# Six weight tiles decoded by an integer addition, ScalarE passes bound to set places, and two foldings split by VectorE

## The chip, the cores and the metric

The kernel runs on one core of one Trainium2 chip. The metric is the device time of one execution in microseconds. Of before three executions were timed: 1432.74, 1432.77 and 1434.7 us, median 1432.77.

## The reference

Attention over eight batches and eight heads, with keys and values first condensed to 32 memory slots, and behind it two feed-forward layers:

```python
a = exp(phi - max(phi, axis=2)); a = a / (sum(a, axis=2) + 1e-9)
k_m = einsum('bhsm,bhsd->bhmd', a, k)
v_m = einsum('bhsm,bhsd->bhmd', a, v)
scores = (q @ k_m.T) / sqrt(64)
attn = softmax(scores)                      # over 32 slots
x = (attn @ v_m) as [4608, 512]
g = x @ w_gate;  x = (silu(g) * (x @ w_val)) @ w_out      # 512 -> 1536 -> 512
h = x @ w_in;    out = elu(h) @ w_out2                     # 512 -> 2048 -> 512
```

q, k, v are 8 x 8 x 576 x 64, phi is 8 x 8 x 576 x 32. The weights come to the chip as 64-bit floating-point words, seen as pairs of 32-bit words.

## The kernel before

The kernel is written in a tile framework: Python functions record instructions, and a scheduler sets the order in which they stand on each engine, by data dependences, by `tc.high_priority()`, and by `tc.issue_after(x)`, which keeps what is recorded in it behind instruction x. Once built, that order is fixed: each engine takes its own list row by row, and waits at a row until the rows of other engines that it needs have ended.

Every matrix product of the feed-forward layers is taken in two parts, an upper part rounded to a short format and the remainder, as three products (upper by upper, upper by lower, lower by upper). So a value that goes into them is split: ScalarE copies it rounded (hi), VectorE subtracts that from it (lo).

Stage 1, some 340 us, goes over the eight batches. Per batch there are front tasks (`phi`: maximum and exponentials of phi; `a_T`: transpositions of them on TensorE into `ps_aT`, copied by ScalarE to `a`, L348 and L342; `kv_mm` and `kv_T`: the condensed keys and values) and back tasks for each half of the batch's positions (`score`; `soft` and `norm`: a softmax on VectorE with its exponential L424 on ScalarE; `attn`: a transposition L451 and the split of the weights into `at`, hi L453 on ScalarE and lo L454 on VectorE). `vw` folds the values into the gate and value weights on TensorE (`pvw`, L237) and splits the result (`vw`, hi L242 on ScalarE, lo L243 on VectorE). `gate1` and `val1` then make the hidden units (`pg` and `pv`, L255 to L257; the gate's activation `s` L279 on ScalarE and L280 on VectorE; `h` L287, split into `hh` L266 and `hl` L268), and `down1` multiplies them with the output weights (`pd`, L260 to L262; copied out by ScalarE L542 and sent to memory, L543). The loop over batches records these products, and `tick()` puts tasks of the next batches, from the list `todo`, between them. Two foldings stand before the loop's own list: (0, 0) ahead of it, (0, 1) within its first products. Stages 2 and 3 are long runs of products from about 340 us on.

The weight tiles are decoded from 64-bit words (`words`): ScalarE takes the upper 32-bit word as a float and scales it (L126), which sets the exponent; VectorE shifts it by three (L127), puts the sign back (L128), makes the word's power of two (L130), scales the lower word by it (L131), and the sum is L144. The output-weight tiles are also split (L171 to L173). `later()` keeps the early decodes behind given instructions. Six tiles are decoded ahead of some 65 us: four gate tiles, two of them in halves, and two output-weight tiles.

The foldings (0, 0) and (0, 1) are split without VectorE, for `NEG` is 1: ScalarE copies one half rounded (L246), TensorE adds its product with the negated identity `minus` (L247), ScalarE copies the remainder (L248). Ahead of folding (0, 1) `spin` puts thirteen products that nobody reads (L300) on TensorE.

Of the kernel before, what the change touches and what calls it, by code (L numbers as in the profile page):

```python
# [8 lines left out]
F32 = mybir.dt.float32  # L9
F32R = mybir.dt.float32r  # L10
I32 = mybir.dt.int32
# [15 lines left out]
UA = 4  # L27
# [4 lines left out]
NSET = (NU1 - UA) // 2  # L32
NKV = 5
NQ = 3
NEG = 1


@with_exitstack
def attention_moe_moe(ctx: ExitStack, tc: tile.TileContext, qT, phiT, kv, kv4, w1g, w1o, w2, out):
# [81 lines left out]
    def words(v, r):  # L121
# [9 lines left out]
        stt(out=cf, in0=lo32.bitcast(U32), scalar=2.0 ** -52, in1=cf, op0=ALU.mult, op1=ALU.mult)  # L131
        return cf

    def later():
        st = ExitStack()
        for after in last.get("h"), first.get("ex"):
            if after:
                st.enter_context(tc.issue_after(after.ins))
        return st

    def load_w(v, r):
        with later():
            cf = words(v, r)
            last["sum"] = tt(out=v, in0=v, in1=cf, op=ALU.add)  # L144

# [3 lines left out]
    def load_wg(p, k2, pool, parts=1):  # L149
        t = pool.tile([128, 2, 512], F32, tag="w", name="wg")  # L150
        WG[p][2 * k2], WG[p][2 * k2 + 1] = t[:, 0], t[:, 1]
        r = raw.pop((p, k2), None)
        if r is None:
            r = fetch_w(w1g[p, k2])
        t = t.rearrange("p i c -> p (i c)")
        n = 1024 // parts
        for i in range(parts):
            cs = slice(n * i, n * i + n)
            load_w(t[:, cs], r[:, cs])
        ahead((p, k2))  # L160

    def load_wo(u2, pool):
        hi = pool.tile([128, 2, 512], F32R, tag="w", name="woh")
        lo = (bk_p if u2 else pool).tile([128, 2, 512], F32R, tag="w", name="wol")
        for i in range(2):
            WO[2 * u2 + i] = hi[:, i], lo[:, i]
        hi, lo = (x.rearrange("p i c -> p (i c)") for x in (hi, lo))
        v = work("wv")
        with later():
            cf = words(v, fetch_w(w1o[u2]))  # L170
            act(out=hi, in_=v, func=AF.Copy)  # L171
            tt(out=v, in0=v, in1=hi.bitcast(F32), op=ALU.subtract)
            tt(out=lo, in0=v, in1=cf, op=ALU.add)  # L173

    SET = {}
    stores = []
# [53 lines left out]
    def vw(b, p, pool=None, ps=None):  # L230
        t = VW[b, p] = vx_p.tile([128, 2, 2, 512], F32R, tag="vx", name="vw")
        both = ps or pool.tile([128, 2, 512], F32, tag="at", name="pvw")
        ps = [both[:, g] for g in range(2)]

        def head(j, g):
            r, c = slice(64 * g, 64 * g + 64), slice(32 * j, 32 * j + 32)
            return mm(ps[g][c], lhsT=Bs[b].vt[r, j, :], rhs=WG[p][j][r], start=True, stop=True)  # L237

        together([lambda j=j, g=g: head(j, g) for j in reversed(range(KD)) for g in (1, 0)])
        if b >= NEG or p >= UA // 2:  # L240
            with tc.high_priority() if pool is None else nullcontext():
                act(out=t[:, 0], in_=both, func=AF.Copy)  # L242
                tt(out=t[:, 1], in0=both, in1=t[:, 0].bitcast(F32), op=ALU.subtract)  # L243
            return
        for g in range(2):
            act(out=t[:, 0, g, :], in_=ps[g], func=AF.Copy)  # L246
            mm(ps[g], lhsT=minus, rhs=t[:, 0, g, :], start=False, stop=True, skip_group_check=True)  # L247
            act(out=t[:, 1, g, :], in_=ps[g], func=AF.Copy)  # L248

    def up1(ps, w, c0, at, s0):  # L250
        cs, ss = slice(c0, c0 + 128), slice(s0, s0 + HS)
# [19 lines left out]
    def gate1(b, u, at, s0, silu):  # L271
        pg = ps_gv.tile([128, HS], F32, tag="g", name="pg")
        up1(pg, VW[b, u // 2], 256 * (u % 2), at, s0)
        s = t_p.tile([128, HS], F32, tag="s", name="s")
        if silu:
            last["gate"] = act(out=s, in_=pg, func=AF.Silu)
        else:

            act(out=s, in_=pg, func=AF.Tanh, scale=0.5)  # L279
            stt(out=s, in0=s, scalar=1.0, in1=pg, op0=ALU.add, op1=ALU.mult)  # L280
        return s

# [19 lines left out]
    class Batch:  # L302
# [18 lines left out]
        def phi(self):  # L321
            ph = self.ph
            nmx = fr_p.tile([128, 2], F32, tag="nmx", name="nmx")
            nc.vector.tensor_reduce(out=nmx, in_=ph, op=ALU.max, axis=AX.X, negate=True)
            sm = fr_p.tile([128, 2], F32, tag="sm", name="sm")
            for g in range(2):
                act(out=ph[:, g, :], in_=ph[:, g, :], func=AF.Exp, bias=nmx[:, g:g + 1],
                    accum_out=sm[:, g:g + 1])
            self.rs = fr_p.tile([128, 2], F32, tag="rs", name="rs", bufs=2)
            nc.vector.tensor_scalar_add(out=self.rs, in0=sm, scalar1=1e-9)  # L330
            nc.vector.reciprocal(out=self.rs, in_=self.rs)
# [3 lines left out]
        def a_T(self, c0):  # L335
            if c0 == 0:
                self.a = fr_p.tile([128, 9, 128], F32, tag="a", name="a")
            ps = ps_fr.tile([128, 4, 128], F32, tag="at", name="ps_aT")
            ph = self.ph.rearrange("p g s -> p (g s)")
            if c0 == 4:  # L340
                nc.tensor.transpose(out=ps[:, 0], in_=ph[:, 512:640], identity=ident)
                act(out=self.a[:, 8], in_=ps[:, 0], func=AF.Copy)  # L342
                return
            for i in range(2):
                for g in range(2):
                    s0 = 128 * (c0 + i) + 640 * g
                    nc.tensor.transpose(out=ps[:, 2 * i + g], in_=ph[:, s0:s0 + 128], identity=ident)
            act(out=self.a[:, 2 * c0:2 * c0 + 4], in_=ps, func=AF.Copy)  # L348


        def kv_mm(self, cs, start, stop):
# [22 lines left out]
        def kv_T(self):  # L374
            ps = ps_fr.tile([128, 2, 4, M], F32, tag="at", name="ps_kvT")
            for i in range(2):
                nc.tensor.transpose(out=ps[:, i].rearrange("p j m -> p (j m)"),
                                    in_=self.kvm[:, i].rearrange("p g d -> p (g d)"), identity=ident)
            self.kT = bk_p.tile([128, 4, M], F32, tag="kT", name="kT", bufs=2)
            act(out=self.kT, in_=ps[:, 0], func=AF.Copy)  # L380
            if self.b == 0:
                self.kTd = bk_p.tile([128, 4, 2, M], F32, tag="kTd", name="kTd")
                nc.gpsimd.memset(self.kTd, 0.0)
                for g in range(2):
                    r = slice(64 * g, 64 * g + 64)
                    act(out=self.kTd[r, :, g], in_=ps[r, 0], func=AF.Copy)
            self.vt = vt_p.tile([128, 4, M], F32, tag="vt", name="vt")
            act(out=self.vt, in_=ps[:, 1], func=AF.Copy)

# [43 lines left out]
        def attn(self, hf):  # L435
            if hf == 0:
                self.at = av_p.tile([128, 2, 2, S], F32R, tag="at", name="at")
            if self.b == 0 and hf == 1:
                t = ps_at.tile([128, 2, T], F32, tag="at", name="ps_ex")
                sc = self.sc.rearrange("p g s -> p (g s)")  # L440
                for i in range(2):
                    for g in range(2):
                        c0 = 256 * i + 128 * g
                        nc.tensor.transpose(out=t[:, g, 128 * i:128 * i + 128], in_=sc[:, c0:c0 + 128], identity=ident)
                for g in range(2):
                    c0 = 512 + M * g
                    last["ex"] = nc.vector.transpose(out=t[:, g, 256:HS], in_=sc[:, c0:c0 + M])
                t = t[:, :, :HS]
            else:
                t = bk_p.tile([128, 2, HS], F32, tag="ex", name="ex")  # L450
                last["ex"] = nc.vector.transpose(out=t.rearrange("p g s -> p (g s)"), in_=self.sc.rearrange("p g s -> p (g s)"))  # L451
            hi, lo = (self.at[:, i, :, HS * hf:HS * hf + HS] for i in range(2))
            act(out=hi, in_=t, func=AF.Copy)  # L453
            tt(out=lo, in0=t, in1=hi.bitcast(F32), op=ALU.subtract)  # L454

        def store_at(self):
# [99 lines left out]
    for b in range(B):  # L556
# [1 line left out]
        bk = list(back_tasks(b + 1)) if b + 1 < B else []  # L558
        fr = list(front_tasks(b + 2)) if b + 2 < B else []
        if b == 0:  # L560
            wo = [lambda u=u: load_wo(u, wo_p) for u in range(UA // 2)]
            pair = last["sum"]

            def phi1():
                with tc.issue_after(pair.ins):
                    Bs[1].phi()
                load_q(Bs[1])

            f1 = [phi1] + list(front_tasks(1)) + [lambda: Bs[2].phi()]
            for i in range(max(len(wo), len(f1))):  # L570
                todo += wo[i:i + 1] + f1[i:i + 1]
        if 2 <= b <= 5:
            bk += [lambda: load_wg(2 + (b - 2) // 2, b % 2, wa_p)]
        if b == B - 2:
# [29 lines left out]
        for hf in range(2):  # L604
            for u in range(UA):
# [2 lines left out]
                hs[hf, u] = val1(b, u, Bs[b].at, HS * hf, s, silu)  # L608
                tick()
                if (b, hf, u) == (0, 0, 1):  # L610
                    with tc.issue_after(last["pe"].ins):
                        spin(ps_kv, "at", 13)
                    vw(0, 1, G2)
                if prev:
                    down1(*prev.pop(0))
# [495 lines left out]
```

## Time and profile before

| | |
|---|---|
| median of 3 executions | 1432.77 us |
| the profiled execution | 1434.9 us, its span 1433.1 us |
| TensorE (PE) busy | 1407.0 us, 98% |
| weight loads (PEld) | 1215.3 us |
| VectorE (DVE) busy | 1141.3 us, 80% |
| ScalarE (ACT) busy | 857.7 us, 60% |
| chain that ended last | PE 89%, DMA 5%, DVE 4% |

Busy time is the time in which an engine works at an instruction; the span goes from the first instruction to the last, and 1.8 us of the profiled execution lie around it. The chain that ended last is followed back from the last instruction, at each step to what released it. TensorE's records overlap: a product's record is longer than its distance from the next, which is seen from the starts.

### The profile page before, as it was taken

Reading aid. Unit: us, or ns where it says so; the run is one execution under the profiler, and the core shown is the slowest. Engines: PE = TensorE matmul, PEld = TensorE weight load, DVE = VectorE, ACT = ScalarE, POOL = GpSimd, SP = SyncE. Lnnn points to the kernel's source line nnn. Section 1 sums busy time; section 2 is a strip of 40 time slices with the busy share of each in tenths; the row PEclk is TensorE's granted clock in tenths of the full one; section 3 lists DMA queues with packets and bytes.
Section 4 is the critical chain, followed back from the end, with each engine's and each line's share of the span. In section 5 each row is a group of like instructions: output and inputs, shape, how many; then the busy total and the mean of one; then the engine's idle time right before and its main releaser. Section 6 shows DMA issues by size and latency. Waiting matters only on the chain.

```text
span 1433.1 us, 23220 instructions
## 1 busy us (share of the span) xinstructions
PE 1407.0 (98%) x9269; PEld 1215.3 (85%) x9269; DVE 1141.3 (80%) x1460; ACT 857.7 (60%) x1251; POOL 44.8 (3%) x73
## 2 busy tenths in 40 slices
PE   5999999999999999999999999999999999999998
PEld 4688889988999999999998888888888888888887
DVE  7998887778798886886978578894898488957884
ACT  4665545544466465465657388556866588549843
POOL 0000000000000000000000000000000000000000
PEclk7999999999999999999999999999999999999999
DMA  9887522663789988888889866766676667666653
GB/s 379 316 316 282 193 75 101 220 231 136 259 248 294 298 235 253 255 246 275 280 270 367 279 203 209 268 212 198 204 272 210 202 205 250 228 205 205 208 204 132
DMA packets 89484, 337.65 MB, mean 236 GB/s; under 512 B 9376, under 2 KB 23712, under 8 KB 70048
## 3 DMA queue, kind: packets, MB, share of 16 engines
q1 hardware_dynamic: 55312, 254.04, 51.4%
q10 hardware_dynamic: 26880, 51.39, 9.8%
q0 software_dynamic: 7184, 30.74, 8.9%
q8 instruction: 73, 1.20, 0.3%
q14 instruction: 35, 0.29, 0.1%
HBM read 251.13 MB, written 85.00 MB: 235 GB/s over the span
## 4 chain that ended last, share of the span: by engine, by line
PE 89%; DMA 5%; DVE 4%; issue 1%; ACT 1%; SPq 0%; ACTq 0%; DVEq 0%
PE pu L834 12%; PE pu L833 12%; PE pu L832 12%; PE pd L834 5%; PE pd L833 5%; PE pd L832 5%; PE acc L262 4%; PE acc L260 4%; PE acc L261 4%; PE pv L255 3%; PE pg L255 3%; PE pv L257 3%; PE pv L256 3%; PE pg L257 3%; PE pg L256 3%; DMA wr<-w1g 3%
## 5 line engine op out<-in xcount | busy, mean ns | idle before, releaser
L834 PE MATMUL pu<-xhi,w 128*128 128x512 f32 x672 | 261.5, 389 | 0.0
L833 PE MATMUL pu<-xlo,w 128*128 128x512 f32 x672 | 261.4, 389 | 0.0
L832 PE MATMUL pu<-xhi,w 128*128 128x512 f32 x672 | 261.4, 389 | 0.0
L861 ACT ACTIVATE xhi<-g 128x1024 fp32r<-128x1024 f32 x120 | 126.6, 1058 | 108.4 <-PE pu L834 65.9
L862 DVE TENSOR_TENSOR xlo<-g,xhi 128x1024 fp32r<-128x1024 f32 x120 | 145.2, 1222 | 42.2 <-ACT xhi L861 42.1
L833 PEld LDWEIGHTS pu<-xlo,w 128*128 128x128 f32 x672 | 126.1, 188 | 26.3
L832 PEld LDWEIGHTS pu<-xhi,w 128*128 128x128 f32 x672 | 126.1, 188 | 26.2
L834 PEld LDWEIGHTS pu<-xhi,w 128*128 128x128 f32 x672 | 126.1, 188 | 26.1
L261 PE MATMUL acc<-hh,ws 128*128 128x288 f32 x448 | 131.8, 296 | 0.0
L260 PE MATMUL acc<-hh,ws 128*128 128x288 f32 x448 | 131.5, 295 | 0.0
L262 PE MATMUL acc<-hl,ws 128*128 128x288 f32 x448 | 128.8, 297 | 0.0
L255 PE MATMUL pv<-at,vw 128*128 128x288 f32 x384 | 116.9, 304 | 3.0 <-DVE s L280 1.2
L255 PE MATMUL pg<-at,vw 128*128 128x288 f32 x384 | 116.5, 303 | 1.9 <-ACT at L453 0.7
L722 ACT ACTIVATE hh<-gh 128x576 fp32r<-128x576 f32 x112 | 76.1, 684 | 67.6 <-PE acc L261 50.3
L257 PE MATMUL pv<-at,vw 128*128 128x288 f32 x384 | 114.2, 297 | 0.0
L256 PE MATMUL pg<-at,vw 128*128 128x288 f32 x384 | 114.0, 297 | 0.2 <-DVE at L454 0.2
L256 PE MATMUL pv<-at,vw 128*128 128x288 f32 x384 | 114.1, 297 | 0.0
L257 PE MATMUL pg<-at,vw 128*128 128x288 f32 x384 | 113.8, 297 | 0.1
L832 PE MATMUL pd<-xhi,w 128*128 128x512 f32 x288 | 112.0, 389 | 0.0
L833 PE MATMUL pd<-xlo,w 128*128 128x512 f32 x288 | 112.0, 389 | 0.0
L834 PE MATMUL pd<-xhi,w 128*128 128x512 f32 x288 | 112.0, 389 | 0.0
L852 DVE SCALAR_TENSOR_TENSOR et<-et 128x1024 f32<-128x1024 f32 x72 | 87.9, 1221 | 28.8 <-ACT et L851 28.8
(154 smaller groups left out, 3240.4 us busy)
## 6 DMA issues: line engine op xcount, KB each, us to landing
w<-dnd SPq DMA_DIRECT2D x64, 1024.0 KB, 5.0
w<-upd SPq DMA_DIRECT2D x40, 1024.0 KB, 5.7
w<-upd SPq DMA_DIRECT2D x32, 768.0 KB, 4.7
ws<-d1d SPq DMA_DIRECT2D x42, 512.0 KB, 5.0
kvr<-kv SPq DMA_DIRECT2D x32, 512.0 KB, 8.2
wr<-w SPq DMA_DIRECT2D x16, 1024.0 KB, 6.3
upd<-uw ACTq DMA_DIRECT2D x32, 512.0 KB, 6.3
dnd<-uw ACTq DMA_DIRECT2D x32, 512.0 KB, 9.1
```

The lines of the kernel that those rows point to most:

```text
L255: mm(ps, lhsT=wh, rhs=ah, start=g == 0, stop=False)
L256: mm(ps, lhsT=wh, rhs=al, start=False, stop=False)
L257: last["pe"] = mm(ps, lhsT=wl, rhs=ah, start=False, stop=g == 1)
L260: mm(ps, lhsT=w[0][:, ms], rhs=hs[0], start=start, stop=False, skip_group_check=skip)
L261: mm(ps, lhsT=w[1][:, ms], rhs=hs[0], start=False, stop=False, skip_group_check=skip)
L262: mm(ps, lhsT=w[0][:, ms], rhs=hs[1], start=False, stop=stop, skip_group_check=skip)
L832: mm(ps, lhsT=w[0], rhs=x[0], start=start, stop=False, skip_group_check=skip)
L833: mm(ps, lhsT=w[0], rhs=x[1], start=False, stop=False, skip_group_check=skip)
L834: last["mm"] = mm(ps, lhsT=w[1], rhs=x[0], start=False, stop=stop, skip_group_check=skip)
L852: stt(out=a, in0=e, scalar=1.0, in1=a, op0=ALU.add, op1=ALU.mult)
L861: last["hi"] = act(out=hi, in_=x, func=AF.Copy)
L862: last["lo"] = tt(out=lo, in0=x, in1=hi.bitcast(F32), op=ALU.subtract)
```

## The change

`words_int` decodes the early tiles: ScalarE makes two passes, one over the upper words as before (L139 in the changed file) and one that turns the lower words into integers (L141); VectorE shifts the first (L142), adds the second as integers (L143) and puts the sign on by and/or (L144). An output-weight tile is then split by ScalarE (L189) and one VectorE row (L190). `BEHIND` binds the ScalarE passes to named instructions: behind an exponential, the `a` copy, `vt`, `at`. `NEG` is 0, so the first two foldings are split like all others (L259 on ScalarE, L260 on VectorE), and the split of every folding of stage 1 is recorded behind the last `ex`. `spin` is no longer called. In the first batch's `todo` the output weights are fetched apart from their decode.

```diff
-NEG = 1
+NEG = 0
...
+    def words_int(v, r, one, two):
+        lo32, hi32 = r[:, :, 0], r[:, :, 1]
+        vi = v.bitcast(I32)
+        n = work("wn").bitcast(I32)[:, :r.shape[1]]
+        with tc.issue_after(last[one].ins) if one else nullcontext():
+            act(out=v, in_=hi32.bitcast(F32), func=AF.Copy, scale=2.0 ** -112)
+        with tc.issue_after(last[two].ins) if two else nullcontext():
+            act(out=n, in_=lo32.bitcast(U32), func=AF.Copy, scale=2.0 ** -29)
+        nc.vector.tensor_scalar(out=vi, in0=vi, scalar1=3, scalar2=None, op0=ALU.logical_shift_left)
+        tt(out=vi, in0=vi, in1=n, op=ALU.add)
+        return stt(out=vi, in0=hi32, scalar=-2 ** 31, in1=vi, op0=ALU.bitwise_and, op1=ALU.bitwise_or)
...
+    BEHIND = {(0, 0): [(None, None), (None, "exp")], (0, 1): [(None, "a2"), (None, None)],
+              (1, 0): [("vt", "vt")], (1, 1): [("at", "at")]}
...
-            cf = words(v, fetch_w(w1o[u2]))
+            words_int(v, raw.pop(("wo", u2)), *[("exp", "s")[u2]] * 2)
             act(out=hi, in_=v, func=AF.Copy)
-            tt(out=v, in0=v, in1=hi.bitcast(F32), op=ALU.subtract)
-            tt(out=lo, in0=v, in1=cf, op=ALU.add)
+            tt(out=lo, in0=v, in1=hi.bitcast(F32), op=ALU.subtract)
...
-            with tc.high_priority() if pool is None else nullcontext():
-                act(out=t[:, 0], in_=both, func=AF.Copy)
+            with tc.high_priority() if pool is None else tc.issue_after(last["ex"].ins):
+                last["vw"] = act(out=t[:, 0], in_=both, func=AF.Copy)
                 tt(out=t[:, 1], in0=both, in1=t[:, 0].bitcast(F32), op=ALU.subtract)
...
-            wo = [lambda u=u: load_wo(u, wo_p) for u in range(UA // 2)]
+            wo = [lambda: (load_wo(0, wo_p), fetch_wo(1)), lambda: load_wo(1, wo_p)]
...
-            for i in range(max(len(wo), len(f1))):
-                todo += wo[i:i + 1] + f1[i:i + 1]
+            todo += [lambda: fetch_wo(0), f1[0], lambda: None, wo[0], f1[1], f1[2], wo[1]] + f1[3:]
...
                 if (b, hf, u) == (0, 0, 1):
-                    with tc.issue_after(last["pe"].ins):
-                        spin(ps_kv, "at", 13)
                     vw(0, 1, G2)
```

The order of the built programs, first on ScalarE in the first batch, from the gates' activations of the first half to the second `a` copy (`ph`: exponentials of phi for batch 1; `wv`, `wn`: decode passes of an output-weight tile; `wr`: its fetched words; `woh`: its upper part). Before:

```order
L266 ACTIVATE hh<-h 128x288
L327 ACTIVATE ph,sm<-ph,nmx 128x576 x2
L266 ACTIVATE hh<-h 128x288
L246 ACTIVATE vw<-pvw 128x512
L348 ACTIVATE a<-ps_aT 128x512
L248 ACTIVATE vw<-pvw 128x512
L246 ACTIVATE vw<-pvw 128x512
L453 ACTIVATE at<-ps_ex 128x2x288
L348 ACTIVATE a<-ps_aT 128x512
```

And now:

```order
L344 ACTIVATE ph,sm<-ph,nmx 128x576 x2
L139 ACTIVATE wv<-wr 128x1024
L141 ACTIVATE wn<-wr 128x1024
L283 ACTIVATE hh<-h 128x288
L259 ACTIVATE vw<-pvw 128x1024
L365 ACTIVATE a<-ps_aT 128x512
L470 ACTIVATE at<-ps_ex 128x2x288
L365 ACTIVATE a<-ps_aT 128x512
```

Two decode passes now stand between the exponentials and the folding's split; before, the tile's one pass stood ahead of the exponentials.

Second, ScalarE some 40 us later, within the first batch's down products, where batch 2's phi is transposed (`a`) and batch 1's second half goes through its softmax (`sc`, `at`; `p`: down products on their way out). Before:

```order
L348 ACTIVATE a<-ps_aT 128x512
L543 DMA p1d_124<-p_894 128x288
L424 ACTIVATE sc<-sc 128x576
L542 ACTIVATE p_957<-pd 128x288
L348 ACTIVATE a<-ps_aT 128x512
L543 DMA p1d_124<-p_957 128x288
L453 ACTIVATE at<-ex 128x2x288
L242 ACTIVATE vw<-pvw 128x1024
L266 ACTIVATE hh<-h 128x288
L279 ACTIVATE s<-pg 128x288
L342 ACTIVATE a<-ps_aT 128x128
```

And now:

```order
L365 ACTIVATE a<-ps_aT 128x512
L441 ACTIVATE sc<-sc 128x576
L559 ACTIVATE p_1007<-pd 128x288
L560 DMA p1d_124<-p_1007 128x288
L470 ACTIVATE at<-ex 128x2x288
L259 ACTIVATE vw<-pvw 128x1024
L365 ACTIVATE a<-ps_aT 128x512
L296 ACTIVATE s<-pg 128x288 x2
L359 ACTIVATE a<-ps_aT 128x128
```

The second `a` copy of four transpositions stood ahead of `at` and the split, and now stands behind both.

Third, TensorE at the same place, around the last transposition of batch 2's phi (`ps_aT<-ident,ph` of 128x128 alone). Before:

```order
L255 MATMUL pv<-at,vw 128x288
L256 MATMUL pv<-at,vw 128x288
L257 MATMUL pv<-at,vw 128x288
L341 MATMUL ps_aT<-ident,ph 128x128
L260 MATMUL pd<-hh,woh 128x288
L261 MATMUL pd<-hh,wol 128x288
```

And now:

```order
L274 MATMUL pv<-at,vw 128x288
L428 MATMUL ps_sc<-qr,kT 32x288 x8
L272 MATMUL pg<-at,vw 128x288
L273 MATMUL pg<-at,vw 128x288
L274 MATMUL pg<-at,vw 128x288
L272 MATMUL pg<-at,vw 128x288
L273 MATMUL pg<-at,vw 128x288
L274 MATMUL pg<-at,vw 128x288
L358 MATMUL ps_aT<-ident,ph 128x128
L272 MATMUL pv<-at,vw 128x288
```

The transposition that needs the second copy done followed the value products, with down products behind it; now a score and the gate products of one unit stand right ahead of it, and value products behind it.

## Rows read from the trace of the kernel before

**Rows 1.** Windows: from:to and its length, then busy time of each engine, clock, DMA.

```profile
60.00:100.00 40.00, 39.21 (x492) 30.24 (x492) 40.00 (x81) 24.54 (x56) 0.00 (x0) 0.98 0.93 346
100.00:200.00 100.00, 99.47 (x1113) 85.32 (x1113) 83.29 (x164) 54.48 (x128) 0.00 (x0) 1.00 0.58 206
400.00:1400.00 1000.00, 999.76 (x5588) 863.56 (x5588) 797.17 (x881) 638.05 (x815) 39.52 (x58) 1.00 0.74 243
```

**Rows 2.** Windows of 10 us, the same columns.

```profile
30.00:40.00 10.00, 8.80 (x34) 7.56 (x33) 10.00 (x14) 2.80 (x6) 0.00 (x0) 0.61 1.03 409
40.00:50.00 10.00, 8.37 (x127) 6.29 (x129) 9.58 (x19) 7.25 (x16) 0.00 (x0) 1.00 0.46 166
```

**Rows 3.** Source views of the decode lines: minimum, median and maximum in ns.

```profile
L126 ACT ACTIVATE wg<-wr x14: 658/1132/1161, 5.1 to 325.1; 128x1024 f32<-128x1024 f32 x10, 128x512 f32<-128x512 f32 x4
...
L127 DVE TENSOR_SCALAR wc<-wg x14: 419/686/694, 5.8 to 326.3; 128x1024 int32<-128x1024 int32 x10, 128x512 int32<-128x512 int32 x4
...
L144 DVE TENSOR_TENSOR wg<-wg,wc x14: 684/1219/1225, 9.6 to 331.3; 128x1024 f32<-128x1024 f32 x10, 128x512 f32<-128x512 f32 x4
```

**Rows 4.** Timeline of TensorE: start, duration, then the instruction.

```profile
36.37 3.80 PE L300 MATMUL spin<-minus 128*128 128x512 f32 x13
40.22 1.09 PE L237 MATMUL pvw<-wg,vt 64*32 64x512 f32 x16
...
43.68 0.29 PE L255 MATMUL pg<-at,vw 128*128 128x288 f32 x1
```

**Rows 5.** Timeline of VectorE and ScalarE around the second folding.

```profile
38.28 1.23 DVE L144 TENSOR_TENSOR wg<-wg,wc 128x1024 f32<-128x1024 f32 x1
...
45.80 0.75 DVE L454 TENSOR_TENSOR at<-ps_ex,at 128x576 fp32r<-128x576 f32 x1
...
42.72 0.58 ACT L246 ACTIVATE vw<-pvw 128x512 fp32r<-128x512 f32 x1
```

**Rows 6.** Timeline of TensorE: the groups of products later, by their starts.

```profile
74.48 0.72 PE L411 MATMUL ps_sc<-qr,kT 64*32 64x288 f32 x16
75.13 0.40 PE L260 MATMUL pd<-hh,woh 128*128 128x288 f32 x1
...
76.83 0.60 PE L347 MATMUL ps_aT<-ident,ph 128*128 128x128 f32 x4
77.36 1.09 PE L237 MATMUL pvw<-wg,vt 64*32 64x512 f32 x16
78.38 0.40 PE L255 MATMUL pg<-at,vw 128*128 128x288 f32 x1
...
80.06 0.28 PE L341 MATMUL ps_aT<-ident,ph 128*128 128x128 f32 x1
```

**Rows 7.** Timeline of ScalarE at the second excerpt's place.

```profile
77.19 0.69 ACT L424 ACTIVATE sc<-sc 128x576 f32<-128x576 f32 x1 [1.60 <-DVE sc L423]
...
78.07 0.59 ACT L348 ACTIVATE a<-ps_aT 128x512 f32<-128x512 f32 x1
...
78.91 0.69 ACT L453 ACTIVATE at<-ex 128x576 fp32r<-128x576 f32 x1 [0.25 <-DVE ex L451]
79.50 1.01 ACT L242 ACTIVATE vw<-pvw 128x1024 fp32r<-128x1024 f32 x1
```

**Rows 8.** Timeline of VectorE: rows of one softmax.

```profile
79.80 0.84 DVE L416 STREAM_TRANSPOSE sc<-ps_sc 128x288 f32<-128x288 f32 x2
...
82.40 0.74 DVE L422 TENSOR_REDUCE mx<-sc 128x18 f32<-128x576 f32 x1
83.06 0.26 DVE L431 RECIPROCAL smx<-smx 128x18 f32<-128x18 f32 x1
...
83.90 0.76 DVE L423 TENSOR_TENSOR sc<-sc,mx 128x576 f32<-128x576 f32 x1
...
86.86 0.78 DVE L451 STREAM_TRANSPOSE ex<-sc 128x576 f32<-128x576 f32 x1
87.55 0.71 DVE L429 TENSOR_REDUCE smx<-sc 128x18 f32<-128x576 f32 x1
```

More of the change, by code (lines that the diff above doesn't have):

```diff
@@ L139, in later, with load_w @@
         return st
-    def load_w(v, r):
+    BEHIND = {(0, 0): [(None, None), (None, "exp")], (0, 1): [(None, "a2"), (None, None)],
+              (1, 0): [("vt", "vt")], (1, 1): [("at", "at")]}
+    def load_w(v, r, behind=None):
         with later():
+            if behind:
+                last["sum"] = words_int(v, r, *behind)
+                return
             cf = words(v, r)
@@ L158, in load_wg @@
             cs = slice(n * i, n * i + n)
-            load_w(t[:, cs], r[:, cs])
+            load_w(t[:, cs], r[:, cs], BEHIND[p, k2][i] if p < UA // 2 else None)
         ahead((p, k2))
@@ L247, in vw @@
             mm(ps[g], lhsT=minus, rhs=t[:, 0, g, :], start=False, stop=True, skip_group_check=True)
-            act(out=t[:, 1, g, :], in_=ps[g], func=AF.Copy)
+            last["vw"] = act(out=t[:, 1, g, :], in_=ps[g], func=AF.Copy)
     def up1(ps, w, c0, at, s0):
@@ L277, in gate1 @@
         else:
-            act(out=s, in_=pg, func=AF.Tanh, scale=0.5)
+            last["s"] = act(out=s, in_=pg, func=AF.Tanh, scale=0.5)
             stt(out=s, in0=s, scalar=1.0, in1=pg, op0=ALU.add, op1=ALU.mult)
@@ L326, in phi @@
             for g in range(2):
-                act(out=ph[:, g, :], in_=ph[:, g, :], func=AF.Exp, bias=nmx[:, g:g + 1],
-                    accum_out=sm[:, g:g + 1])
+                last["exp"] = act(out=ph[:, g, :], in_=ph[:, g, :], func=AF.Exp, bias=nmx[:, g:g + 1],
+                                  accum_out=sm[:, g:g + 1])
             self.rs = fr_p.tile([128, 2], F32, tag="rs", name="rs", bufs=2)
@@ L347, in a_T @@
                     nc.tensor.transpose(out=ps[:, 2 * i + g], in_=ph[:, s0:s0 + 128], identity=ident)
-            act(out=self.a[:, 2 * c0:2 * c0 + 4], in_=ps, func=AF.Copy)
+            last["a2"] = act(out=self.a[:, 2 * c0:2 * c0 + 4], in_=ps, func=AF.Copy)
         def kv_mm(self, cs, start, stop):
@@ L387, in kv_T @@
             self.vt = vt_p.tile([128, 4, M], F32, tag="vt", name="vt")
-            act(out=self.vt, in_=ps[:, 1], func=AF.Copy)
+            last["vt"] = act(out=self.vt, in_=ps[:, 1], func=AF.Copy)
         def score(self, hf):
@@ L452, in attn @@
             hi, lo = (self.at[:, i, :, HS * hf:HS * hf + HS] for i in range(2))
-            act(out=hi, in_=t, func=AF.Copy)
+            last["at"] = act(out=hi, in_=t, func=AF.Copy)
             tt(out=lo, in0=t, in1=hi.bitcast(F32), op=ALU.subtract)
@@ L560, in attention_moe_moe, with fetch_wo @@
         if b == 0:
-            wo = [lambda u=u: load_wo(u, wo_p) for u in range(UA // 2)]
+            def fetch_wo(u2):
+                raw["wo", u2] = fetch_w(w1o[u2])
+            wo = [lambda: (load_wo(0, wo_p), fetch_wo(1)), lambda: load_wo(1, wo_p)]
             pair = last["sum"]
```

## The prediction

> **What bounds the kernel now.** The windows view came first [rows 1]: behind 400 us TensorE is busy 999.76 us of 1000, so nothing that this change touches can be won or lost there; whatever TensorE loses ahead of 400 us it carries unshortened to the end. Between 60 and 100 us it is busy 39.21 of 40 us while VectorE is busy all 40.00, and between 100 and 200 us TensorE is at 99.47 of 100. So the margin ahead of 200 us is thin: TensorE waits little, but VectorE has no slack for 40 us, and a result that comes late there is a stall. The 10 us windows [rows 2] show the stage before: the granted clock is 0.61 between 30 and 40 us and 1.00 in the next ten, and TensorE is busy 8.80 and 8.37 of 10 us. Then I read the source views of the decode lines [rows 3] and the timelines of single stretches [rows 4 to 8].
>
> **What the change removes and adds.** Decode of a tile of 1024 words on VectorE before: L127 0.68 us, L128, L130 0.68, L131, L144; L128 and L131 are two-input rows of the shape of L144 and are put at its 1.22 us [rows 3]: 3 x 1.22 + 2 x 0.68 = 5.02 us. After: the shift 0.68, the integer add L143, the and/or L144 1.22. No row of before is an integer add on two tensors. It is bounded below by the cheapest 1024-word row, 0.68, and above by two rows of L144, 2.44, because the printed order gives it twice the words (128x2048). I take 1.22, the row with two inputs of 1024 words, so 3.12 us a tile. The Trainium skill ("VectorE: DVE Perf Modes", Specifications) says that integer operands are converted and are exact only below 2^24; these words are larger, so by this rule the add can't be the plain two-input row. Its table (The perf-mode tier table) has 2293 ns for a two-input row of 2048 fp32 words, and the sum by that price would be that of my upper bound; no row here shows which holds.
>
> Four gate tiles save 1.90 us each (the two cut in halves somewhat less, 2.93 to 1.81 a half); the two output-weight tiles also lose one of two splitting rows, 5.02 + 2 x 1.22 to 3.12 + 1.22, 3.12 us each. The split of two foldings adds 2 x 1.22 to VectorE. In all VectorE is freed of about 9.6 us ahead of 60 us. ScalarE gets a second decode pass a tile (the row of 1.13 us, 0.66 for a half [rows 3]), 7.3 us, and loses two half-tile passes of 0.58 us [rows 5] against one longer one in each of two foldings, so gains about 4.6 us. TensorE loses thirteen idle products of 3.80 us together and the four products with the negated identity.
>
> **What of it reaches TensorE early.** The second folding (pvw) began at 40.22 us, behind the last decode row that began at 38.28 and took 1.23 [rows 4, 5]. Two whole tiles with 1.90 us less each bring that decode to its end some 3 us sooner, at about 36.4 us. But the gain is lost within ScalarE's order (first pair of excerpts): before, one small pass (hh) stood between the exponentials and the first piece of the folding's split; now two decode passes stand there, 2 x 1.13 us, then the full split of 1.00. Placing every row of the printed order behind the row ahead of it and behind the rows that it waits for, with the durations of before, the first gate product of the second folding comes at 43.9 us against 43.68 [rows 4], and the lower half of the attention weights ends at 46.4 us against 45.80 + 0.75 = 46.55 [rows 5]. At 60 us the kernel is between 0.3 and 1.7 us ahead, depending on the clock.
>
> That clock is the second unknown. Before, it stood at 0.61 between 30 and 40 us and at 1.00 in the next ten [rows 2], with the thirteen products from 36.37 to 40.2 us [rows 4]. Without them the full clock can come as before, or with the dense products behind 45 us, at about 51 us. The first gives 1.7 us at 60 us, the second 0.3; half clock to 61.7 us would cost 5 us more in the end than the first. I take the second. The Trainium skill ("TensorE: Matmul & The Clock Gate", Part 1) says that the throttled clock is the default and activity releases it, which speaks against taking the idle products out; that is the 1.6 us between the two cases.
>
> **What the new order does behind 60 us.** Nothing between 60 and 400 us is decoded differently, but the order printed for each engine is another one in all of stage 1. I laid the two orders side by side, row by row, as above (for before this gives 254.18 us for a VectorE row that the trace has at 255.06; TensorE's lost time between 62 and 100 us comes out at 3.3 us by the rows and 2.9 by the trace's own starts, between 62 and 200 us at 6.4 and 7.3). The stalls that come out of the changed order are larger, and one can be followed by hand.
>
> In the excerpts from ScalarE, later in the program, before has both `a` copies (L348) ahead of `at` (L453), and the trace shows it so: the copy at 78.07, `at` at 78.91, the split at 79.50 [rows 7]. In the changed order the second `a` copy stands behind `at` L470 and the split L259. `at` ends a whole chain on VectorE and ScalarE. TensorE's next transposition (L358, third pair of excerpts) waits for the second copy. Count from the moment when the previous split's upper half is done. TensorE has until L358: twelve down products (75.13 to 76.83 with one slow one, so 1.6 to 1.7 us), eighteen gate and value products (twelve took 78.38 to 80.06, so 2.4), one folding (77.36 to 78.38, 1.02), four transpositions (76.83 to 77.36, 0.45 to 0.53) and a score (74.48 to 75.13, 0.65) [rows 6]: 6.1 us. The other side has the split's lower half, a two-input row of 1024 words, 1.22 [rows 3], two transpositions 0.84, maximum 0.74, subtraction 0.76, exponential 0.69, sum 0.71, two short rows (0.26 the longer), a scaling like the subtraction 0.76, the 576-wide transposition 0.78, `at` 0.69, the split 1.01, the copy 0.59 [rows 7, 8], with overlaps at the hand-overs: 9.4 us. So TensorE stands 9.4 - 6.1 = 3.3 us, at about 87 us, where in the trace of before all its idle time from 60 to 100 us is 0.79 us [rows 1].
>
> The second largest: on VectorE the changed order puts three softmax rows (scaling 0.76, two transpositions 0.84, the wide transposition 0.78) and a maximum 0.74 ahead of the gate's row `s` (L297), for whose buffer the next gate product waits: 2.2 us at 109 us. Others of the same kind: 1.5 us (161 us), 1.4 (76), 1.1 (167, 270 and 313), 1.0 (88) and a dozen under 1 us. In the order of before two exceed 0.7 us. By stages, changed minus before: -0.3 at 60 us, +3.1 at 100, +7.6 at 200, +10.5 at 300, +12.9 at 400, and unchanged from there. VectorE's freed time helps nothing here, because the chain waits for its turn on ScalarE. The loads cost nothing: on SP's queue they stand in the same order as before up to the second batch's, but for two neighbours that change places.
>
> **The sum.** 1434.9 us is the profiled execution, 1.8 us of it outside its span; the median of the runs is 2.1 us below it. Early -0.3, order +13.2: 12.9 us. With the integer add at 0.68 the same rows give +9.7 to +11.8, at 2.44 +15.5 to +16.4; clock early +11.3, half to 61.7 us +16.2. Between the middle and the dearer add I take 13.2: 1434.9 + 13.2 = 1448.1 for an execution like the profiled one, and **1446 us** against the median.
>
> **Rivals.** *The saving stays* (faster): hand-overs in the new order hurt no more than in the old one. Then only the early gain counts, and it decides from the point where the `a` copy comes before TensorE wants it: that is 0.3 to 1.7 us at 60 us, or up to 3.8 us if the idle products' whole time comes back: 1429 to 1432.5 us. For it speaks that TensorE loses only 0.79 us of busy time between 60 and 100 us now; against it that the copy's place in the order is fixed and the chain cannot be shorter than its rows. Chance of faster by over 0.2% (2.9 us, about what a measurement of this kernel tells from no change): 0.07; within it 0.07. *Half the stalls*: the rows overlap better than placed, and the losses behind 60 us are 5 to 8 us: 1437 to 1441 us. Chance 0.16. *The dear add or the late clock*: VectorE is full to 100 us [rows 1], so six adds at 2.44 cost 7.3 us there, of which about 3 show: 1448 to 1452 us. Chance 0.25. The forecast itself, 1441 to 1448, has 0.43; the 0.02 left is for over 1452.
>
> Range 1438 to 1451: below it lie the gain, no change and the mildest stalls, above it the worst of the dear cases. Slower by over 0.2%: 0.86.
>
> **What would show it.** In the profile after: TensorE's busy time between 60 and 200 us at least 5 us lower than now; an idle of 2 to 4 us ahead of the transposition L358 near 87 us, ended by ScalarE's `a`; one of about 2 us near 109 us, ended by VectorE's `s`; the second folding near 37 us and its gate products near 44; 400 to 1400 us as full as now. The row of L143 settles the add. Wrong would be the forecast if ScalarE's `a` copies came in time in spite of their place, if the full clock between 20 and 50 us returned sooner without the idle products, or if loads that I take as landed in time (those moved behind the output weights' fetches) came late.

## The result and the profile after

The changed kernel takes 1443.79 us, the median of 4 executions (1442.45 to 1445.05), against 1433.01 for before (4 executions): a ratio of 1.0073, with a 95% interval from 1.0055 to 1.009. It is some 10.8 us slower; 1446 was forecast, with a range from 1438 to 1451. The profiled execution took 1443.84 us, its span is 1442.1, 9.0 us over that of before.

The windows of the changed kernel, with the columns of [rows 1]:

```profile
30.00:40.00 10.00, 6.52 (x37) 4.20 (x36) 10.00 (x16) 3.09 (x7) 0.00 (x0) 0.67 1.03 410
40.00:50.00 10.00, 8.19 (x43) 7.32 (x42) 7.23 (x14) 8.07 (x14) 0.00 (x0) 0.65 0.46 175
60.00:100.00 40.00, 35.23 (x430) 27.37 (x429) 34.85 (x69) 22.81 (x52) 0.00 (x0) 0.91 0.86 309
100.00:200.00 100.00, 97.73 (x1034) 83.44 (x1033) 82.92 (x161) 53.55 (x123) 0.00 (x0) 1.00 0.59 208
200.00:400.00 200.00, 196.24 (x1651) 178.01 (x1651) 156.91 (x243) 96.66 (x181) 1.22 (x2) 1.00 0.49 174
400.00:1400.00 1000.00, 999.76 (x5615) 865.00 (x5614) 800.54 (x890) 637.87 (x817) 40.42 (x59) 1.00 0.75 243
```

Behind 400 us TensorE (first column) is as busy as before to the hundredth. Against [rows 1] it lost 3.98 us of busy time between 60 and 100 us (39.21 to 35.23) and 1.74 between 100 and 200. VectorE, full between 60 and 100 us before, is busy 34.85 of 40 us now: it is no longer full, and TensorE lost time all the same. Between 200 and 400 us the row of before is

```profile
200.00:400.00 200.00, 197.26 (x1580) 181.08 (x1579) 157.93 (x243) 97.94 (x179) 2.11 (x3) 1.00 0.52 180
```

so another 1.0 us is lost there: 6.7 us of busy time in all behind 60 us. Against [rows 2] the granted clock between 40 and 50 us is 0.65 in place of 1.00.

Three rows tell what the early part came to, the second folding and its first gate product on TensorE:

```profile
36.90 1.96 PE L254 MATMUL pvw<-wg,vt 64*32 64x512 f32 x16 [1.96 <-DVE wg L144]
...
43.82 0.61 PE L272 MATMUL pg<-at,vw 128*128 128x288 f32 x1 [1.52 <-ACT vw L259]
```

and the lower half of the attention weights on VectorE:

```profile
45.95 0.74 DVE L471 TENSOR_TENSOR at<-ps_ex,at 128x576 fp32r<-128x576 f32 x1
```

Against [rows 4, 5] the folding starts 3.3 us sooner (36.90 against 40.22), the gate product is level (43.82 against 43.68), and the lower half too (46.69 against 46.55). ScalarE's passes between them took the gain. The folding, 1.96 us long where it took 1.09, was done at 38.86, and its split L259 began only at 42.77, behind the exponentials and two decode passes on ScalarE:

```profile
40.39 1.13 ACT L139 ACTIVATE wv<-wr 128x1024 f32<-128x1024 f32 x1
41.42 1.10 ACT L141 ACTIVATE wn<-wr 128x1024 int32<-128x1024 uint32 x1
...
42.77 1.00 ACT L259 ACTIVATE vw<-pvw 128x1024 fp32r<-128x1024 f32 x1
```

The price that no row of before showed is in the source view of the integer addition (duration in ns, minimum, median, maximum):

```profile
L143 DVE CUSTOM_DVE_ANT_0 wg<-wg,wn x6: 691/694/1217, 6.3 to 32.2; 128x1024 uint16<-128x1024 uint16 x4, 128x2048 uint16<-128x2048 uint16 x2
...
L143 DVE CUSTOM_DVE_ANT_0 wv<-wv,wn x2: 1207/1210/1214, 43.7 to 53.3; 128x2048 uint16<-128x2048 uint16 x2
```

1.21 us for a whole tile, 0.69 for a half. It is recorded over 2048 16-bit elements, and takes what L144 takes for 1024 words of 32 bits [rows 3].

The stall that the prediction followed by hand is in the timeline of TensorE:

```profile
82.43 0.29 PE L274 MATMUL pg<-at,vw 128*128 128x288 f32 x1
85.37 0.47 PE L358 MATMUL ps_aT<-ident,ph 128*128 128x128 f32 x1 [2.64 <-ACT a L365]
86.50 0.61 PE L272 MATMUL pv<-at,vw 128*128 128x288 f32 x1 [0.66 <-DVE s L297]
```

and ScalarE at the same place:

```profile
74.39 0.68 ACT L470 ACTIVATE at<-ex 128x576 fp32r<-128x576 f32 x1
74.97 1.02 ACT L259 ACTIVATE vw<-pvw 128x1024 fp32r<-128x1024 f32 x1
...
83.23 0.68 ACT L470 ACTIVATE at<-ex 128x576 fp32r<-128x576 f32 x1 [2.64 <-DVE ex L468]
83.82 1.00 ACT L259 ACTIVATE vw<-pvw 128x1024 fp32r<-128x1024 f32 x1
84.72 0.59 ACT L365 ACTIVATE a<-ps_aT 128x512 f32<-128x512 f32 x1
```

TensorE stands 2.64 us until the second `a` copy, which comes behind `at` and the split as the order has them; then 0.66 us more for the gate's `s`. And a second loss follows, in windows cut at the clock's steps (the clock is the third column from the right):

```profile
77.70:84.40 6.70, 5.03 (x56) 3.17 (x54) 5.00 (x9) 2.15 (x4) 0.00 (x0) 1.00 0.95 362
84.50:91.30 6.80, 5.28 (x71) 4.25 (x72) 6.26 (x13) 3.12 (x8) 0.00 (x0) 0.50 0.48 148
```

From 84.5 to 91.3 us the granted clock is 0.50, the lower of its two levels, 1.2 GHz; before, the clock was full there. The part of this stretch in which TensorE worked would have taken up to half of 5.28 us less at the full one. (Counted from 0, the copies are those of batch 3's phi in both traces, not batch 2's as the text ahead of the prediction has it. And the two excerpts of ScalarE show different softmaxes: `at` at 78.91 us in [rows 7] is batch 1's second half, which here ran at 74.39, ahead of both copies; `at` at 83.23 is the next one, batch 2's first half. So the second copy, ahead of the one softmax before, stands behind both now.)

### The profile page after: what moved, and what is told of

It reads as the page before. It is cut to its first block, busy times and chain, and to the rows that moved or that the text cites. A ratio compares the mean times of both kernels' runs of the same rounds, so it can differ in the third digit from the quotient of the medians.

```text
span 1442.1 us, 23167 instructions
## 1 busy us (share of the span) xinstructions
PE 1404.4 (97%) x9252; PEld 1212.7 (84%) x9252; DVE 1137.3 (79%) x1446; ACT 862.4 (60%) x1253; POOL 44.8 (3%) x73
## 4 chain that ended last, share of the span: by engine, by line
PE 86%; DVE 7%; DMA 4%; ACT 2%; issue 1%; SPq 0%; DVEq 0%; ACTq 0%
PE pu L851 12%; PE pu L850 12%; PE pu L849 12%; PE pd L851 5%; PE pd L850 5%; PE pd L849 5%; PE acc L279 4%; PE acc L277 4%; PE acc L278 4%; PE pg L272 3%; PE pv L272 3%; PE pv L274 3%; PE pv L273 3%; DMA wr<-w1g 3%; PE pg L274 3%; PE pg L273 3%
```

## The experiments

The theory: the changed orders on the engines make the loss, stage by stage, whatever the operations cost. Rivals: the early work itself costs the time, or the clock that comes later without the idle products. Every kernel was timed beside the kernel before.

**One copy ahead (e1).** The copy of one attention half, bound behind the `a` copy:

```diff
-            last["at"] = act(out=hi, in_=t, func=AF.Copy)
+            with tc.issue_after(last["a2"].ins) if (self.b, hf) == (2, 0) else nullcontext():
+                last["at"] = act(out=hi, in_=t, func=AF.Copy)
```

> The changed kernel with one edit: the ScalarE copy of one attention half (the one in the excerpt, L470) is bound behind the `a` copy before it, so that the copy stands ahead of it on ScalarE. Theory of the order: the stall of 2.6 us before the transposition L358 near 85 us goes, and with it may go the half clock that follows it from 84.5 to 91.3 us; from the printed rows 2.4 to 2.7 us less than the changed kernel (about 1441), up to 6 us less (1438) if the half clock goes too. Rival, the early stage's work itself (decode passes, no idle products) makes the loss: within 1 us of the changed kernel, 1443 to 1445, since the stall only moves.

Measured: 1440.95 us (1440.79 to 1444.08), ratio 1.0051, from 1.0035 to 1.0068. The median falls by 2.8 us, as the rows have it, but the interval overlaps that of the changed kernel, and TensorE's timeline shows something else than was expected:

```profile
85.72 0.40 PE L272 MATMUL pv<-at,vw 128*128 128x288 f32 x1 [2.49 <-DVE s L297]
```

The stall at L358 is gone, and 2.49 us stand one step later, at the value products, which wait for the gate's `s`: this too is behind the same chain on ScalarE. So the stall mostly moved, 2.49 us in place of 2.64 and 0.66, and the half clock behind it is shorter: the clock's records have it from 86.8 to 90.2 us here. The profile was taken in the slowest of the four executions, 1444.08 us; the other three took 1440.8 to 1441.1. This run alone decides little.

**The orders put back (e2, e3, e4).** e2 restores the first batch's list of tasks; e3 takes the split's binding off; e4 does both.

```diff
-            wo = [lambda: (load_wo(0, wo_p), fetch_wo(1)), lambda: load_wo(1, wo_p)]
+            wo = [lambda u=u: (fetch_wo(u), load_wo(u, wo_p)) for u in range(UA // 2)]
...
-            todo += [lambda: fetch_wo(0), f1[0], lambda: None, wo[0], f1[1], f1[2], wo[1]] + f1[3:]
+            for i in range(max(len(wo), len(f1))):
+                todo += wo[i:i + 1] + f1[i:i + 1]
...
-            with tc.high_priority() if pool is None else tc.issue_after(last["ex"].ins):
+            with tc.high_priority() if pool is None else nullcontext():
```

> The changed kernel with the first batch's list of tasks put back as before (fetch and decode of an output-weight tile together, alternating with the front tasks); decode, split and missing idle products stay changed. Theory of the order: by the rows in the printed order 3.6 to 4.8 us over before, 1436.5 to 1438. Rival, the work itself costs the time: within 2 us of the changed kernel, 1442 to 1446. Rival, the clock without idle products: the same as the changed kernel, since nothing that raises the clock is added.

> The changed kernel without the binding of every folding's split behind the last wide transposition (`ex`); all else stays changed. Theory of the order: 5.3 to 5.6 us over before by the printed rows, 1438 to 1439. Rivals (the work itself, or the clock without idle products): 1442 to 1446.

> The changed kernel with both of these edits: the list of tasks as before and the split not bound. Integer decode, its ScalarE bindings, the split by VectorE and the missing idle products stay. Theory of the order: from 2.2 us under to 1.0 us over before by the printed rows, 1431 to 1434. Rivals (the work itself, or the clock without idle products): not under 1440.

Measured: e2 1438.02 us (ratio 1.0034, from 1.0021 to 1.0048), at the upper end of what the rows say; e3 1443.08 (1.0063, from 1.0046 to 1.008), 4 us over what they say; e4 1435.05 (1.001, from 0.9999 to 1.002), 1 us over their upper end. All operations of the change are still in e4, and 8.7 of its 10.8 us are gone: by themselves neither the work nor the missing idle products cost that. But e4 does not part the order from the early clock, which came sooner with it. Of e4 between 40 and 50 us, and of e2 and the kernel before from 50 to 400 us:

```profile
40.00:50.00 10.00, 9.20 (x128) 7.87 (x126) 8.47 (x18) 5.97 (x11) 0.00 (x0) 1.00 0.66 229
```

```profile
50.00:400.00 350.00, 339.77 (x3221) 299.58 (x3220) 287.77 (x491) 184.07 (x374) 2.11 (x3) 1.00 0.59 210
```

```profile
50.00:400.00 350.00, 344.11 (x3254) 303.37 (x3243) 289.90 (x500) 185.15 (x379) 2.11 (x3) 1.00 0.60 212
```

e4 has the full clock there without idle products, where the changed kernel has 0.65. e2 has it from 50 to 400 us, and its TensorE is idle for 10.2 us there against 5.9 in before: waiting costs without any half clock in that stretch. e3 misses the rows, and its profile has stalls of its own. Between 60 and 110 us the longest of TensorE's waits is (total, times, longest)

```profile
PE ps_kvT L394 <- ACT kvm L388: 3.2, 1, 3.2
```

and behind it, from 77.72 us on, the clock stays full:

```profile
77.80:82.00 4.20, 3.57 (x46) 2.13 (x47) 3.26 (x5) 2.53 (x5) 0.00 (x0) 1.00 0.87 343
```

In e4 the executions spread from 1432.57 to 1438.35 us. Its profile, taken in the slowest, shows a stall that may be part of the reason; no faster execution of it was profiled. ScalarE:

```profile
178.48 1.12 ACT L126 ACTIVATE wg<-wr 128x1024 f32<-128x1024 f32 x1 [2.17 <-DMA wr<-w1g]
...
179.83 0.40 ACT L559 ACTIVATE p<-pd 128x288 f32<-128x288 f32 x1
```

and TensorE:

```profile
177.87 0.29 PE L274 MATMUL pv<-at,vw 128*128 128x288 f32 x1
180.28 0.40 PE L277 MATMUL pd<-hh,woh 128*128 128x288 f32 x1 [2.12 <-ACT p L559]
...
180.89 0.45 PE L277 MATMUL pd<-hh,woh 128*128 128x288 f32 x1
181.13 0.45 PE L278 MATMUL pd<-hh,wol 128*128 128x288 f32 x1
```

A decode pass of a later weight tile (L126) stands at the head of ScalarE's list and waits 2.17 us for its load. `p` stands behind it, and TensorE waits 2.12 us for the buffer that `p` frees. From 180.7 us on the products are 0.24 us apart in place of 0.13: half clock again.

**The idle products (e5, e7).** e5 puts the thirteen products back into the changed kernel, e7 takes them out of the kernel before:

```diff
                 if (b, hf, u) == (0, 0, 1):
-                    with tc.issue_after(last["pe"].ins):
-                        spin(ps_kv, "at", 13)
                     vw(0, 1, G2)
```

> The changed kernel with the thirteen idle products put back where they were; all else stays changed. They also change the order that the scheduler makes of what follows. Theory of the order: by the printed rows 5.2 us over before if the full clock comes at 37.8 us as before, 7.0 if it comes at 47, so 1438 to 1440.5. Rival, the clock without idle products is the cause: full clock from about 38 us on, no half clock near 85 us, and within 2 us of before, 1431 to 1435. Rival, the early work: 1442 to 1446.

> The kernel before without the thirteen idle products, nothing else. Theory of the order: the products themselves hide behind the decode; their absence changes the order behind, 3.6 to 4.4 us over before by the printed rows, 1436.5 to 1437.5, and the full clock comes later than 37.8 us. Rival, the idle products cost what they last: 3 to 4 us under before, 1429 to 1430.

Measured: e5 1438.3 us (1435.78 to 1443.03; ratio 1.0043, from 1.0027 to 1.0059), within the order's range; e7 1440.77 (1.0056, from 1.0041 to 1.0071), 3 us over it. The windows of e5:

```profile
35.00:50.00 15.00, 10.48 (x139) 7.69 (x138) 12.94 (x25) 10.48 (x19) 0.00 (x0) 1.00 0.67 255
70.00:100.00 30.00, 27.20 (x327) 20.61 (x325) 27.55 (x52) 19.43 (x43) 0.00 (x0) 1.00 0.86 321
```

and of e7:

```profile
35.00:50.00 15.00, 10.44 (x70) 7.51 (x69) 13.81 (x23) 9.06 (x18) 0.00 (x0) 0.66 0.60 242
70.00:100.00 30.00, 28.51 (x320) 22.35 (x318) 27.65 (x56) 18.73 (x44) 0.00 (x0) 0.94 0.83 291
```

With the products the clock is full from 35 to 100 us (in the fastest of e5's five executions, the one profiled); without them it is 0.66 between 35 and 50 us, and 0.94 between 70 and 100 because it fell once more, from 85.3 to 88.7 us, behind waits of 1.22 and 0.27 us. A longer wait of e7 left it full:

```profile
151.75 0.40 PE L260 MATMUL pd<-hh,woh 128*128 128x288 f32 x1 [2.27 <-ACT p L542]
```

```profile
152.00:156.00 4.00, 3.89 (x30) 3.66 (x30) 3.83 (x9) 3.05 (x8) 0.00 (x0) 1.00 0.12 44
```

The expectation of e7 had priced the later rise, not this second fall. So by the medians the idle products are worth 5.5 us in the changed kernel (the intervals of e5 and of the changed kernel just touch) and 7.7 in the one before, part of it by the order that the scheduler makes with them; order and clock can't be told apart in these two runs.

**One part alone (e6, e11).** e6 is the kernel before with `words_int` for the six tiles and nothing else (the passes of the two output-weight tiles are bound in it too); e11 is the kernel before with

```diff
-NEG = 1
+NEG = 0
```

> The kernel before with the integer decode of the six tiles alone: ScalarE passes not bound, idle products in, the two foldings split as before through TensorE, the split not bound, the list of tasks as before. Theory of the order: by the printed rows 0.9 us over before (full clock at 37.8 us) to 4.2 (at 47 us), so 1434 to 1438; what VectorE saves, some 9 us, does not show. Rival, that the decode is worth what it frees on VectorE: 2 us or more under before, 1426 to 1431.

> The kernel before with the first two foldings split by ScalarE and VectorE instead of through TensorE, nothing else (idle products in). Theory of the order: VectorE, which is full to 100 us, gets 2.4 us more and the order behind changes: 6.5 to 7.1 us over before by the printed rows, 1439.5 to 1440. Rival, the split moves four products off TensorE and shortens the way to the first gate products: 0 to 2 us under before, 1431 to 1433.

Measured: e6 1436.74 us (ratio 1.0024, from 1.0015 to 1.0034), as expected; e11 1438.07 (1.0035, from 1.0021 to 1.0048), 1.5 to 2 us under what the rows said, and no gain. Each part alone costs time in the old surroundings: the decode 3.7 us, the split 4.9, the missing idle products 7.7. Their sum, 16 us, is over the 10.8 of all together, so they don't add.

**Without the gate tiles' bindings (e8) and the late pass (e9, e10).** e8 is e4 without the bindings of the gate tiles' decode passes (`BEHIND` names nothing; the passes of the two output-weight tiles stay bound); e9 and e10 bind the pass L126 of the later tiles behind `at` or `s`:

```diff
-        act(out=v, in_=hi32.bitcast(F32), func=AF.Copy, scale=2.0 ** -112)
+        with tc.issue_after(last["at"].ins):
+            act(out=v, in_=hi32.bitcast(F32), func=AF.Copy, scale=2.0 ** -112)
```

> The run with list of tasks and split as before (e4), and the decode's ScalarE passes not bound to named instructions either: what stays changed is the integer decode, the split of the first two foldings by VectorE and the missing idle products. Theory of the order: from 1.5 us under before to 1.8 over by the printed rows, 1431 to 1435, with some spread where a decode pass on ScalarE waits for its tile's load. Rival, that the bindings are what makes the decode cheap: more than e4, over 1437.

> The run without bindings (e8), and one edit: ScalarE's decode pass of the later gate tiles (L126) is bound behind the last `at`, so that the pass of the tile fetched at 48.78 us no longer stands ahead of `kvm` on ScalarE while its load has not landed. Theory: the stall of 2.7 us before the transposition of `kvm` at 64.6 us goes, and the half clock behind it (64.9 to 68.3 us) with it, some 4 us at 70 us; a part is lost later by the order (2.3 us by the printed rows between 80 and 200 us). So 1430 to 1432, 1 to 3 us under before. Rival, any new order loses as much elsewhere: 1433 to 1436.

> As the run before this one, with the pass bound behind the last gate activation `s` instead. Theory: the same stall gone, the rest of the order a little other, by the printed rows 1.2 us slower than the one bound behind `at`: 1431 to 1433. Rival: 1433 to 1436.

Measured: e8 1433.45 us (ratio 1.0, from 0.9991 to 1.0009), as the rows said. ScalarE in e8:

```profile
62.90 1.12 ACT L126 ACTIVATE wg<-wr 128x1024 f32<-128x1024 f32 x1 [2.54 <-DMA wr<-w1g]
63.92 0.62 ACT L387 ACTIVATE kvm<-ps_kvm,rs 128x128 f32<-128x128 f32 x2
```

and TensorE:

```profile
64.59 0.44 PE L393 MATMUL ps_kvT<-ident,kvm 128*128 128x128 f32 x2 [2.74 <-ACT kvm L387]
64.96 1.96 PE L253 MATMUL pvw<-wg,vt 64*32 64x512 f32 x16
```

The pass waits 2.54 us for its load with `kvm` behind it, TensorE waits 2.74 us for `kvm`, and the folding that follows takes 1.96 us where it took 1.09 [rows 6]: half clock. The window of e8, and that of e9:

```profile
60.00:70.00 10.00, 7.05 (x61) 4.09 (x55) 7.88 (x15) 5.56 (x12) 0.00 (x0) 0.83 1.02 415
```

```profile
60.00:70.00 10.00, 8.64 (x102) 6.75 (x94) 8.58 (x17) 6.34 (x14) 0.00 (x0) 1.00 1.02 415
```

With the pass bound later the clock stays at 1.00 and TensorE is busy 8.64 us in place of 7.05. e9 measured 1432.08 us (0.9992, from 0.9983 to 1.0001), e10 1432.7 (0.9995, from 0.9986 to 1.0004): the stall and the half clock went as said, e9 came out at the upper edge of its range and e10 within it. They are 1.4 and 0.8 us under e8, and neither is clear of before or of e8.

**Only the turns (e12).** From e10, with no operation added or taken away:

```diff
-        spread = 18 if b == 0 else 16 if b < B - 2 else 24
+        spread = 16 if b == 0 else 16 if b < B - 2 else 24
...
-            upto = min(len(todo), -(-len(todo) * (done[0] + (3 if b else -1)) // spread))
+            upto = min(len(todo), -(-len(todo) * (done[0] + (2 if b else -1)) // spread))
```

> The run with the late pass bound behind `s` (e10), and the task list's pace changed alone: the first batch's tasks are spread over 16 turns instead of 18, those of the later batches start one turn later. No operation is added or taken away. Theory of the order: by the printed rows 4.3 us less than e10, so 1428 to 1430, 3 to 5 us under before. Rival, what is left is the work's own, and the order is worth no more: within 1.5 us of e10, 1431 to 1434.

Measured: 1431.16 us against 1434.11 for before beside it, ratio 0.9979, from 0.997 to 0.9989. This is the one version that is clearly faster than the kernel before, by 3 us, with the integer decode and without idle products. Against before that is the low end of the 3 to 5 us expected; in microseconds it missed 1428 to 1430 and lies within the rival's 1431 to 1434, and its interval overlaps that of e10. So e12 shows that these operations can beat before; that its turns gained over e10 is not shown clear of the noise. Its windows:

```profile
100.00:200.00 100.00, 98.93 (x1111) 84.96 (x1110) 83.47 (x164) 54.74 (x127) 0.00 (x0) 1.00 0.58 204
200.00:400.00 200.00, 199.03 (x1604) 182.14 (x1603) 161.00 (x244) 101.78 (x182) 2.12 (x3) 1.00 0.53 184
```

TensorE is busy 98.93 and 199.03 us, where the changed kernel has 97.73 and 196.24.

## Why the prediction was right

**The direction and its cause** held: the loss comes from the order, most of it behind 60 us. With every operation of the change kept, other orders gave 1431 to 1443 us (e2, e3, e4, e8 to e10, e12). Of the signs named ahead, TensorE's busy time between 60 and 200 us fell by 5.7 us (at least 5 were said), and 400 to 1400 us is as full as before.

**The early part** held in its places: folding 36.90 us (36.4 forecast), gate product 43.82 (43.9), lower half done 46.69 (46.4). Full clock came at about 47 us by the clock records, between the two cases that were weighed.

**VectorE's freed time**, put at 9.6 us, came to 9.7: the decode rows of the six tiles, with the output weights' split, took 34.2 us before and take 22.1 now, and two more foldings' splits take 2.4. The terms named for it give 11.4, though: the 3.12 us of an output-weight tile count a row L144 that such a tile does not have (1.9 by the trace), and a tile in halves saves 2.2 us, more than a whole one and not less.

**The integer addition** measured 1.21 us, the middle value taken; the dear case, 2.44 us, is out. Of the two figures that the Trainium skill has for 2048 elements ("VectorE: DVE Perf Modes", The perf-mode tier table) the trace, which records a custom instruction over 16-bit elements, agrees with the one for bf16, 1224 ns, by 1207 to 1217 ns, and not with the one for fp32, 2293 ns, which the prediction had quoted.

**The stall by hand** was 3.3 us near 87; it is 2.64 us ahead of 85.37, ended by the copy as forecast, and 0.66 more behind it, ended by `s`. The chain came out as placed: from the end of the previous split's upper half (74.97 + 1.02 = 75.99 us) to 85.37 it took 9.4 us, 9.4 forecast. The other side was put too small: TensorE's work until then took 6.7 us, from 75.99 to the end of the product at 82.43, not 6.1. The eighteen gate and value products, put at 2.4 us, took 2.9 in their three groups (76.04 to 76.67, 79.80 to 81.03 and 81.67 to 82.72).

**Mis-sized** were the stalls later on. 2.2 us were forecast at 109 us; all waits of TensorE for `s` between 100 and 200 us are

```profile
PE pg L272 <- DVE s L297: 1.1, 2, 0.6
```

1.1 us in two. Between 100 and 200 us the forecast had +4.5 us and 1.74 of busy time were lost, between 200 and 400 us it had +5.3 and 1.0 were lost. Placed row by row, small delays add up, and in the trace most of them did not reach TensorE.

**Missing** was the half clock from 84.5 to 91.3 us, up to 2.6 us: the prediction weighed the clock ahead of 60 us alone. It made up for part of the oversized stalls.

**Luck** brought 1446 closer to 1443.8 than its terms deserve. For an execution like the profiled one 13.2 us over before were forecast, and the two traces differ by 9.0. Of this miss of 4.2 us 2.1 do not show against the medians, because the profiled execution of before was one of its slower ones (1434.9 against 1432.77) and that of the changed kernel was not (1443.84 against 1443.79).

**Not settled**: how the 10.8 us divide between clock and waiting. In the traces TensorE waits 6.7 us more behind 60 us, and the half clock near 85 us cost up to 2.6 (before has up to 0.8 of the same kind in the 0.98 of [rows 1]); so waiting is the larger part there. How much of it the half clock and the early clock bring about is open: e1 was meant for it and did not tell, and in e4, e8 to e10 and e12 the order and the early clock changed together.

## What to carry to other kernels

Where one engine is the bound and others feed it just in time, relieving a feeder gains nothing if the new order puts a long chain, or a pass that waits for a load, ahead of a short copy that the bound engine needs: read in the built order what stands ahead of each such copy. Build and time several orders of the same operations before judging the operations; here they spread over 12 us, from clearly slower than before to clearly faster. And a wait on TensorE may cost more than its length: in the changed kernel, e1, e4 and e8 the clock fell during or just behind one of 2 to 3 us, though in e3 and e7 it did not behind 3.15 and 2.27.

## What the runs showed of the hardware that was not expected

A VectorE addition over 2048 16-bit elements took 1.21 us, as long as one over 1024 32-bit words. During or just behind TensorE's waits of 2.64 us (changed kernel), 2.49 (e1), 2.12 (e4) and 2.74 (e8) the granted clock fell to half; in the kernel before without idle products (e7) it fell behind 1.22 and 0.27 us. Yet it stayed full behind 2.27 us in e7 and behind 3.15 in e3: the length of a wait alone did not tell which. The Trainium skill ("TensorE: Matmul & The Clock Gate", Part 1) has the throttled clock as the default that activity releases; the trace agrees in so far as e5 with idle products kept the full clock from 35 to 100 us and the changed kernel without them had 0.65 between 40 and 50 us, but e4 had 1.00 there without them too.
